# Delivering most of the input already transposed by DMA, behind the first weights, in a linear-attention and GEGLU kernel

## The chip, the cores and the metric

The kernel runs on one core of a Trainium2 chip. The metric is the device time of one execution in microseconds (us), as the median of several executions; all runs compared here are of the same ("fast") state unless the text says otherwise. The profiled execution's span is about 1.7 us shorter than its device time.

## The reference, cut to what matters

```python
S, D, H, F = 2048, 640, 32, 1728           # tokens, width, heads, FFN width; all bf16
g = sigmoid((x * gate_w).sum(-1, keepdims=True))
# A: linear attention
q, k, v = split_heads(x @ wqkv)            # head dim 20
phi = lambda t: where(t > 0, t + 1, exp(t)) + 1e-6
kv, z = sum_s(phi(k) v^T), sum_s(phi(k))   # over ALL tokens
a = ((phi(q) @ kv) / (phi(q) . z)) @ wo
# B: GEGLU
b = (gelu(x @ w_gate) * (x @ w_up)) @ w_down
out = g * a + (1 - g) * b
```

Every product contracts over the width D, so x is needed with D on the partitions: x transposed (`xT`, 5 blocks of 128 by 2048 tokens). The K and V projections of all 16 token tiles come first, because kv and z sum over all tokens.

## The kernel before

It is a hand-scheduled program: `op`, `mmg` and `dma` issue an instruction on an engine and insert semaphore waits from a table of readers and writers. x is cut in four chunks of 512 tokens. All loads go through one queue, that of SyncE (SP).

```python
for q in range(4):                                   # 4 x 640 KB, natural layout
    dma([], [r_xnat[q]], (sem_x[q], 16), ... x_nat[:, 4*q:4*q+4, :] <- x2[q*512:(q+1)*512, :] ...)
dma(... gwrow <- gate_w ...)                         # 1.2 KB
dma([], [r_wkv], (sem_wkv, 16), ... wkv_sb <- A_wqkv[:, D:3*D] ...)   # 1600 KB
for q in range(4): sp.wait_ge(sem_x[q], 16)
# ... then wo, wq, w_gate, w_up, w_down (8 MB) ...

for gi, (c, k) in enumerate(tgroups):                # 4 chunks x 5 blocks, 8 PSUM banks in turn
    bank = gi % 8
    mmg([r_xnat[c], r_ident], [r_bank[bank]], [4 transposes 128x128 into pt (bf16 PSUM)])
    op(DV, [r_bank[bank]], [r_xT[k][c]], lambda e: e.tensor_copy(xT[:, k, c*512:(c+1)*512], pt[...]))
# ... gate_w transposed the same way ...

for t in range(NT):                                  # 16 token tiles: the KV phase
    # 3 groups (512, 512, 256 columns) x 5 matmuls into banks 3*(t%2) .. 3*(t%2)+2
    mmg(xT_chunk(t // TPC) + [r_wkv], banks3, emits)
    # ScalarE: exp and relu of K, copy of V;  VectorE: min, add -> pk_sb, v_sb
    if t == 3:
        emit_gate_row()                              # 20 matmuls, reads ALL of xT
# then: mask matmuls into banks 4, 5, 6;  kv^T = 5 x 16 matmuls;  z;  q;  W2;  FFN and output, 4 chunks
```

## Time and profile before

| | before |
|---|---|
| median of runs | 331.55 us (330.78 to 333.22, 16 runs) |
| profiled span | 329.7 us |
| TensorE busy | 313.5 us, 95% of the span |
| first TensorE instruction | 5.09 us |
| first KV matmul | 14.95 us |

The page's row of slices first (the span in 40 equal parts, each 8.2 us; a digit is the busy share in tenths, `PEclk` the granted TensorE clock in tenths, `GB/s` what the DMA engines moved).

```profile
...
PE   3699999799999999999999999999999999999996
...
PEclk9999999999899999999999999999999999999999
DMA  7999300000000000000000000000000100000001
GB/s 255 379 392 388 111 1 1 2 2 0 0 2 0 0 1 3 35 27 20 0 2 0 0 22 20 34 9 1 1 2 0 40 22 20 0 3 1 20 22 40
DMA packets 9489, 15.46 MB, mean 47 GB/s; under 512 B 442, under 2 KB 7546, under 8 KB 9466
...
```

Four slices of TensorE are not nearly full: the first two (3 and 6), the eighth (7), and the last (6), the end of the kernel. The DMA engines are busy in the first four slices only. From the third slice on the kernel is mostly bound by TensorE, so only the start can be gained by a change to the loads. The timeline of the start says what happens there (columns: start, duration in us, engine, line, operation, output <- input, number merged, and in brackets the idle time before it with what ended it).

```profile
...
0.80 2.43 SPq L292 DMA_DIRECT2D x_nat<-in_A_x_dram  x4
...
3.79 0.38 SPq L311 DMA_DIRECT2D wkv_sb<-in_A_wqkv_dram  x1
...
5.09 6.89 PE L354 MATMUL pt<-ident,x_nat 128*128 128x128 bf16 x80 [5.09 <-DMA x_nat<-in_A_x_dram]
5.74 7.67 DVE L360 COPY xT<-pt 128x512 bf16<-128x512 bf16 x20 [5.74 <-PE pt L354]
...
14.95 10.76 PE L435 MATMUL ps<-wkv_sb,xT 128*128 128x512 bf16 x58 [2.87 <-DMA wkv_sb<-in_A_wqkv_dram]
17.64 0.70 ACT L445 ACTIVATE e1k<-ps 128x640 bf16<-128x640 f32 x1 [15.56 <-PE ps L435]
...
```

The four x loads are issued at 0.80 us, wkv (`L311`) at 3.79 us. The transposes start when the first x chunk has landed (5.09 us) and end at 11.98 us. Then TensorE idles for 2.87 us until wkv has landed, and the KV phase starts at 14.95 us. The chain of waits (followed back from the last instruction; start, duration, what) agrees:

```profile
...
3.79 10.81 DMA wkv_sb<-in_A_wqkv_dram
...
```

wkv takes 10.81 us from issue to landing, because 2.6 MB of x are ahead of it in the queue.

### The profile page before, as it was taken

To read this page: it belongs to the slowest core of one execution; us is meant where nothing else is said; L and a number is where in the kernel's file an instruction comes from. 1 tells how busy PE (TensorE), PEld (TensorE's weight loads), DVE (VectorE), ACT (ScalarE), POOL (GpSimd) and SP (SyncE) were. 2 spreads that over 40 slices of the span, in tenths; PEclk is the share of its full clock that TensorE was granted. 3 is DMA by queue.
4 is the path that set the end of the run, shared out by engine and by line. 5 is a ranking of instruction groups with operands and counts; after the bars stand their busy time and mean duration, and the time that the engine had idled before them with its cause. 6 is when DMAs were issued, how large, how long until landed. Compare 5 with 4: busy or idle time off the path is not lost.

```text
span 329.7 us, 4747 instructions
## 1 busy us (share of the span) xinstructions
PE 313.5 (95%) x1795; PEld 168.9 (51%) x1819; DVE 192.0 (58%) x320; ACT 165.9 (50%) x318; POOL 73.5 (22%) x64
## 2 busy tenths in 40 slices
PE   3699999799999999999999999999999999999996
PEld 3555555554444445564444555544445564444664
DVE  3625222216869995712999954079995712999400
ACT  1067677618577873104777600267873105777111
POOL 8000000000026540000654300026540000666000
PEclk9999999999899999999999999999999999999999
DMA  7999300000000000000000000000000100000001
GB/s 255 379 392 388 111 1 1 2 2 0 0 2 0 0 1 3 35 27 20 0 2 0 0 22 20 34 9 1 1 2 0 40 22 20 0 3 1 20 22 40
DMA packets 9489, 15.46 MB, mean 47 GB/s; under 512 B 442, under 2 KB 7546, under 8 KB 9466
## 3 DMA queue, kind: packets, MB, share of 16 engines
q1 hardware_dynamic: 9466, 15.16, 12.7%
q8 instruction: 14, 0.23, 0.3%
q14 instruction: 9, 0.07, 0.1%
HBM read 12.54 MB, written 2.62 MB: 46 GB/s over the span
## 4 chain that ended last, share of the span: by engine, by line
PE 78%; DVE 7%; issue 6%; ACT 4%; DMA 3%; SPq 1%; ACTq 0%; DVEq 0%
PE ps L736 20%; PE ps L637 14%; PE ps L435 13%; PE ps L643 12%; PE ps L727 7%; PE ps L467 5%; DMA wkv_sb<-in_A_wqkv_dram 3%; DVE t L680 3%; ACT xh L657 2%; PE ps L551 2%; PE ps L596 1%; PE ps L561 1%; PE ps L497 1%; DVE inner L664 1%; ACT rq L475 1%
## 5 line engine op out<-in xcount | busy, mean ns | idle before, releaser
L688 POOL TENSOR_TENSOR uT<-u,omg_bc 128x512 bf16<-128x512 bf16 x48 | 66.0, 1374 | 225.4 <-DVE u L684 225.4
L664 DVE SCALAR_TENSOR_TENSOR inner<-sq,xh 128x512 bf16<-128x512 bf16 (+1 forms) x56 | 49.4, 882 | 44.2 <-ACT xh L657 43.9
L736 PE MATMUL ps<-wd_sb,uT 128*128 128x320 bf16 x448 | 73.2, 300 | 0.2
L643 PE MATMUL ps<-xT,wu_sb 128*128 128x512 bf16 (+1 forms) x277 | 68.9, 379 | 0.2
L637 PE MATMUL ps<-xT,wg_sb 128*128 128x512 bf16 (+1 forms) x272 | 68.0, 379 | 0.9 <-issue 0.5
L736 PEld LDWEIGHTS ps<-wd_sb,uT 128*128 128x128 bf16 x448 | 42.8, 97 | 26.2 <-issue 4.2
L752 ACT ACTIVATE out_sb<-ps 128x320 bf16<-128x320 f32 x32 | 12.2, 434 | 83.5 <-PE ps L736 83.5
L654 ACT ACTIVATE sq<-ps 128x512 bf16<-128x512 f32 (+1 forms) x56 | 33.4, 596 | 29.7 <-PE ps L637 27.1
L435 PE MATMUL ps<-wkv_sb,xT 128*128 128x512 bf16 (+1 forms) x235 | 43.2, 343 | 3.1 <-DMA wkv_sb<-in_A_wqkv_dram 2.9
L643 PEld LDWEIGHTS ps<-xT,wu_sb 128*128 128x128 bf16 (+1 forms) x280 | 27.6, 99 | 32.8
L637 PEld LDWEIGHTS ps<-xT,wg_sb 128*128 128x128 bf16 (+1 forms) x280 | 27.0, 99 | 33.6 <-ACT sq L654 1.7
L680 DVE SCALAR_TENSOR_TENSOR t<-th,ps 128x512 bf16<-128x512 bf16 (+1 forms) x56 | 37.9, 676 | 0.0
L672 ACT ACTIVATE th<-inner 128x512 bf16<-128x512 bf16 (+1 forms) x56 | 35.3, 630 | 1.0 <-DVE inner L664 1.0
L435 PEld LDWEIGHTS ps<-wkv_sb,xT 128*128 128x128 bf16 x240 | 23.3, 98 | 22.9 <-issue 2.7
L657 ACT ACTIVATE xh<-ps 128x512 bf16<-128x512 f32 (+1 forms) x56 | 33.1, 591 | 0.0
L684 DVE TENSOR_TENSOR u<-t,xh 128x512 bf16<-128x512 bf16 (+1 forms) x56 | 30.0, 535 | 1.9
L727 PE MATMUL ps<-W_sb,pqnT 128*128 128x320 bf16 x160 | 27.0, 299 | 0.0
L445 ACT ACTIVATE e1k<-ps 128x640 bf16<-128x640 f32 x16 | 11.2, 703 | 27.3 <-PE ps L435 27.3
L467 PE MATMUL ps<-xT,wq_sb 128*128 128x512 bf16 x96 | 22.8, 379 | 0.6 <-issue 0.6
L454 DVE TENSOR_SCALAR emk<-e1k 128x640 bf16<-128x640 bf16 x16 | 5.2, 327 | 26.2 <-ACT e1k L445 26.2
L727 PEld LDWEIGHTS ps<-W_sb,pqnT 128*128 128x128 bf16 x160 | 15.7, 98 | 6.1
L480 DVE TENSOR_TENSOR pqT<-emq,rq 128x512 bf16<-128x512 bf16 x20 | 16.1, 807 | 2.0 <-ACT rq L475 1.3
(68 smaller groups left out, 203.2 us busy)
## 6 DMA issues: line engine op xcount, KB each, us to landing
x_nat<-in_A_x_dram SPq DMA_DIRECT2D x4, 640.0 KB, 6.2
out_dram<-out_sb SPq DMA_DIRECT2D x16, 160.0 KB, 1.8
wg_sb<-in_B_w_gate_dram SPq DMA_DIRECT2D x1, 2160.0 KB, 14.5
wu_sb<-in_B_w_up_dram SPq DMA_DIRECT2D x1, 2160.0 KB, 19.4
wd_sb<-in_B_w_down_dram SPq DMA_DIRECT2D x1, 2080.0 KB, 21.7
wkv_sb<-in_A_wqkv_dram SPq DMA_DIRECT2D x1, 1600.0 KB, 10.8
wo_sb<-in_A_wo_dram SPq DMA_DIRECT2D x1, 800.0 KB, 6.3
wq_sb<-in_A_wqkv_dram SPq DMA_DIRECT2D x1, 800.0 KB, 8.1
```

Of the source, the lines that this page charges most:

```text
L435: emits.append(lambda e, base=base, coff=coff, width=width, t=t, k=k: e.matmul(ps[:, base + coff: base + coff + width], lhsT=xT[:, k, t * ...
L467: [lambda e, k=k, i=i, qb=qb: e.matmul(bank_ap(qb), lhsT=wq_sb[:, k, 128 * i:128 * (i + 1)], rhs=xT[:, k, c0:c0 + CH], start=(k == 0), sto ...
L637: [lambda e, k=k, Mj=Mj, f0=f0, gb=gb: e.matmul(bank_ap(gb, p1=Mj), lhsT=wg_sb[:, k, f0:f0 + Mj], rhs=xT[:, k, c0:c0 + CH], start=(k == 0) ...
L643: [lambda e, k=k, Mj=Mj, f0=f0, ub=ub: e.matmul(bank_ap(ub, p1=Mj), lhsT=wu_sb[:, k, f0:f0 + Mj], rhs=xT[:, k, c0:c0 + CH], start=(k == 0) ...
L654: lambda e, Mj=Mj, gb=gb, sl=sl: e.activation(sq[0:Mj, sl, :], bank_ap(gb, p1=Mj), ACT.Square, scale=SQ_SCALE))
L657: lambda e, Mj=Mj, gb=gb, sl=sl: e.activation(xh[0:Mj, sl, :], bank_ap(gb, p1=Mj), ACT.Copy, scale=0.5))
L664: lambda e, Mj=Mj, sl=sl: e.scalar_tensor_tensor(out=inner[0:Mj, sl, :], in0=sq[0:Mj, sl, :], scalar=1.0, in1=xh[0:Mj, sl, :], op0=ALU.add ...
L672: lambda e, Mj=Mj, sl=sl: e.activation(th[0:Mj, sl, :], inner[0:Mj, sl, :], ACT.Tanh, scale=2.0 * GELU_C))
L680: lambda e, Mj=Mj, ub=ub, sl=sl: e.scalar_tensor_tensor(out=t2[0:Mj, sl, :], in0=th[0:Mj, sl, :], scalar=1.0, in1=bank_ap(ub, p1=Mj), op0= ...
L688: lambda e, Mj=Mj, sl=sl, jf=jf, cb=cb: e.tensor_tensor(uT[0:Mj, cb, jf, :], u1[0:Mj, sl, :], omg_bc[0:Mj, c0:c0 + CH], ALU.mult))
L727: lambda e, i=i, bank=bank, coff=coff, mi=mi, cb=cb, tok0=tok0: e.matmul(bank_ap(bank, n=HALF_D), lhsT=pqnT[:, cb, i, tok0:tok0 + 128], rh ...
L736: lambda e, jf=jf, Mj=Mj, bank=bank, coff=coff, mi=mi, cb=cb, tok0=tok0: e.matmul(bank_ap(bank, n=HALF_D), lhsT=uT[0:Mj, cb, jf, tok0:tok0 ...
```

## The change

Its intent: wkv goes ahead of three of the four x chunks; these three come from DRAM already transposed (a transposing DMA straight into `xT`), so TensorE and VectorE transpose only chunk 0. 81 dummy matmuls bridge TensorE's waiting times so that its clock is not lowered. The gate row, which needs all of `xT`, moves from tile 3 to tile 7.

```diff
-for q in range(4): dma(... x_nat chunk q ...)
-dma(gwrow);  dma(wkv)
+dma([], r_W2[0:TPC], (sem_x[0], 16), ... W2_sb[:, 0:4, :] <- x2[0:CH, :] ...)   # chunk 0, natural
+dma(wkv)
+dma(gwrow)
+for c in range(1, NCH):                                   # chunks 1 to 3
+    dma([], [r_xT[k][c] for k in range(KT)], (sem_x[c], 16),
+        lambda e, c=c: e.dma_start_transpose(xT[:, :, c*CH:(c+1)*CH], x2[c*CH:(c+1)*CH, :]))
 for q in range(NCH): sp.wait_ge(sem_x[q], 16)
 # ... wo, wq, w_gate, w_up, w_down as before ...
-for c, k in tgroups (20): 4 transposes into bf16 PSUM, one VectorE copy
+45 dummy matmuls (ident x ident, 128x128) into bank 6
+for k in range(KT):                                       # chunk 0 only: plain matmuls by ident, fp32 PSUM
+    mmg(r_W2[0:TPC] + [r_ident], [r_bank[k]], [4 matmuls lhsT=W2_sb[:, j, k*128:(k+1)*128], rhs=ident])
+    op(DV, [r_bank[k]], [r_xT[k][0]], ... tensor_copy(xT[:, k, 0:CH], bank_ap(k)))
+36 dummy matmuls into bank 6
 # gate_w transposed (now a plain matmul)
 ...
-            if t == 3:
+            if t == 7:
                 emit_gate_row()
```

More of the change, by code (lines that the diff above doesn't have):

```diff
@@ L285, in _build @@
     with nc.Block():
-        xa_x_nat = nc.sbuf_tensor("x_nat", [128, NT, D], dt.bfloat16, side="right")
-        xa_gwrow = nc.sbuf_tensor("gwrow", [KT, 128], dt.bfloat16, side="right")
-        xa_pt = nc.psum_tensor("pt", [128, 8192], dt.bfloat16)
-        with xa_x_nat as x_nat, xa_gwrow as gwrow, xa_pt as pt:
-            for q in range(4):
-                dma([], [r_xnat[q]], (sem_x[q], 16),
-                    lambda e, q=q: e.dma_start(
-                        x_nat[:, 4 * q:4 * q + 4, :],
-                        x2[q * 512:(q + 1) * 512, :].rearrange("(t p) d -> p t d", p=128)))
-            dma([], [r_gwrow], (sem_gw, 16),
-                lambda e: e.dma_start(gwrow[:], gate_w.rearrange("(k p) -> k p", p=128)))
-            esP = ExitStack()
-            esP.__enter__()
-            pk_sb = esP.enter_context(nc.sbuf_tensor("pk_sb", [128, NT, D], dt.bfloat16))
-            v_sb = esP.enter_context(nc.sbuf_tensor("v_sb", [128, NT, D], dt.bfloat16))
-            e1k = esP.enter_context(nc.sbuf_tensor("e1k", [128, 2, D], dt.bfloat16))
-            rk = esP.enter_context(nc.sbuf_tensor("rk", [128, 2, D], dt.bfloat16))
-            emk = esP.enter_context(nc.sbuf_tensor("emk", [128, 2, D], dt.bfloat16))
-            zr_sb = esP.enter_context(nc.sbuf_tensor("zr_sb", [1, D], dt.float32))
-            maskT = esP.enter_context(nc.sbuf_tensor("maskT", [128, KT, 160], dt.bfloat16))
-            KVT_bd = esP.enter_context(nc.sbuf_tensor("KVT_bd", [128, KT, D], dt.bfloat16))
-            wkv_sb = esP.enter_context(nc.sbuf_tensor("wkv_sb", [128, KT, 2 * D], dt.bfloat16))
-            dma([], [r_wkv], (sem_wkv, 16),
-                lambda e: e.dma_start(wkv_sb[:], A_wqkv[:, D:3 * D].rearrange("(k p) f -> p k f", p=128)))
-            for q in range(4):
-                sp.wait_ge(sem_x[q], 16)
-            sp.wait_ge(sem_gw, 16)
-            dma([], [r_wo], (sem_wo, 16),
-                lambda e: e.dma_start(wo_sb[:], A_wo.rearrange("(k p) f -> p k f", p=128)))
-            dma([], [r_wq], (sem_wq, 16),
-                lambda e: e.dma_start(wq_sb[:], A_wqkv[:, 0:D].rearrange("(k p) f -> p k f", p=128)))
-            dma([], [r_wg], (sem_wg, 16),
-                lambda e: e.dma_start(wg_sb[:], B_w_gate.rearrange("(k p) f -> p k f", p=128)))
-            dma([], [r_wu], (sem_wu, 16),
-                lambda e: e.dma_start(wu_sb[:], B_w_up.rearrange("(k p) f -> p k f", p=128)))
-            dma([], [r_wd[0]], (sem_wd, 32),
-                lambda e: e.dma_start(wd_sb[:, 0:FB - 1, :],
-                                      B_w_down[0:(FB - 1) * 128, :].rearrange("(k p) f -> p k f", p=128)))
-            dma([], [r_wd[1]], (sem_wd, 32),
-                lambda e: e.dma_start(wd_sb[0:F - (FB - 1) * 128, FB - 1, :],
-                                      B_w_down[(FB - 1) * 128:F, :]))
-            op(PO, [], [r_ident], lambda e: e.memset(ident[:], 0.0))
-            op(PO, [], [r_ident], lambda e: e.affine_select(
-                out=ident[:], in_=ident[:], compare_op=ALU.not_equal, fill=1.0,
-                base=0, pattern=[[-1, 128]], channel_multiplier=1))
-            op(PO, [], [r_ones], lambda e: e.memset(ones_col[:], 1.0))
-            op(PO, [], [r_ones], lambda e: e.memset(onesF[:], 1.0))
-            op(PO, [], [r_ones], lambda e: e.memset(onesB[:], 1.0))
-            op(PO, [], [r_Ez], lambda e: e.memset(E_sb[:], 0.0))
-            op(PO, [r_Ez], [r_E], lambda e: e.memset(E_sb[0:32, :], 1.0))
-            op(PO, [], [r_E], lambda e: e.affine_select(
-                out=E_sb[0:32, :], in_=E_sb[0:32, :], compare_op=ALU.is_ge, fill=0.0,
-                base=0, pattern=[[1, D]], channel_multiplier=-DH))
-            op(PO, [], [r_E], lambda e: e.affine_select(
-                out=E_sb[0:32, :], in_=E_sb[0:32, :], compare_op=ALU.is_ge, fill=0.0,
-                base=(DH - 1), pattern=[[-1, D]], channel_multiplier=DH))
-            op(PO, [], [r_KVTbd_z], lambda e: e.memset(KVT_bd[:], 0.0))
-            op(PO, [], [r_Zbz], lambda e: e.memset(Zb[:], 0.0))
-            tgroups = [(c, k) for c in range(NCH) for k in range(KT)]
-            for gi, (c, k) in enumerate(tgroups):
-                bank = gi % 8
-                emits = []
-                for j in range(TPC):
-                    t = TPC * c + j
-                    emits.append(lambda e, bank=bank, j=j, t=t, k=k: e.transpose(
-                        pt[:, bank * 1024 + j * 128: bank * 1024 + (j + 1) * 128],
-                        x_nat[:, t, k * 128:(k + 1) * 128],
-                        ident[:]))
-                mmg([r_xnat[c], r_ident], [r_bank[bank]], emits)
-                op(DV, [r_bank[bank]], [r_xT[k][c]],
-                   lambda e, bank=bank, k=k, c=c: e.tensor_copy(
-                       xT[:, k, c * 512:(c + 1) * 512],
-                       pt[:, bank * 1024:bank * 1024 + 512]))
-            gwb = len(tgroups) % 8
-            mmg([r_gwrow, r_ident], [r_bank[gwb]],
-                [lambda e: e.transpose(pt[:, gwb * 1024:gwb * 1024 + KT], gwrow[0:KT, :], ident[0:KT, 0:KT])])
-            op(DV, [r_bank[gwb]], [r_gw],
-               lambda e: e.tensor_copy(gw_sb[:, :], pt[:, gwb * 1024:gwb * 1024 + KT]))
-            snapA = snapshot()
@@ L374, in bank_ap, with emit_xT_dma @@
             return ps[p0:p1, b * 512 + lo:b * 512 + lo + n]
+        def emit_xT_dma(c):
+            dma([], [r_xT[k][c] for k in range(KT)], (sem_x[c], 16),
+                lambda e, c=c: e.dma_start_transpose(
+                    xT[:, :, c * CH:(c + 1) * CH],
+                    x2[c * CH:(c + 1) * CH, :]))
+        gwrow = es.enter_context(nc.sbuf_tensor("gwrow", [KT, 128], dt.bfloat16, side="right"))
+        x_nat = W2_sb[:, 0:TPC, :]
+        dma([], r_W2[0:TPC], (sem_x[0], 16),
+            lambda e: e.dma_start(x_nat, x2[0:CH, :].rearrange("(t p) d -> p t d", p=128)))
@@ new lines, in _build @@
+        esP = ExitStack()
+        esP.__enter__()
+        pk_sb = esP.enter_context(nc.sbuf_tensor("pk_sb", [128, NT, D], dt.bfloat16))
+        v_sb = esP.enter_context(nc.sbuf_tensor("v_sb", [128, NT, D], dt.bfloat16))
+        e1k = esP.enter_context(nc.sbuf_tensor("e1k", [128, 2, D], dt.bfloat16))
+        rk = esP.enter_context(nc.sbuf_tensor("rk", [128, 2, D], dt.bfloat16))
+        emk = esP.enter_context(nc.sbuf_tensor("emk", [128, 2, D], dt.bfloat16))
+        zr_sb = esP.enter_context(nc.sbuf_tensor("zr_sb", [1, D], dt.float32))
@@ new lines, in _build @@
+        maskT = esP.enter_context(nc.sbuf_tensor("maskT", [128, KT, 160], dt.bfloat16))
+        KVT_bd = esP.enter_context(nc.sbuf_tensor("KVT_bd", [128, KT, D], dt.bfloat16))
+        wkv_sb = esP.enter_context(nc.sbuf_tensor("wkv_sb", [128, KT, 2 * D], dt.bfloat16))
+        dma([], [r_wkv], (sem_wkv, 16),
+            lambda e: e.dma_start(wkv_sb[:], A_wqkv[:, D:3 * D].rearrange("(k p) f -> p k f", p=128)))
+        dma([], [r_gwrow], (sem_gw, 16),
+            lambda e: e.dma_start(gwrow[:], gate_w.rearrange("(k p) -> k p", p=128)))
@@ new lines, in _build @@
+        for c in range(1, NCH):
+            emit_xT_dma(c)
+        for q in range(NCH):
+            sp.wait_ge(sem_x[q], 16)
+        sp.wait_ge(sem_gw, 16)
+        dma([], [r_wo], (sem_wo, 16),
+            lambda e: e.dma_start(wo_sb[:], A_wo.rearrange("(k p) f -> p k f", p=128)))
+        dma([], [r_wq], (sem_wq, 16),
+            lambda e: e.dma_start(wq_sb[:], A_wqkv[:, 0:D].rearrange("(k p) f -> p k f", p=128)))
+        dma([], [r_wg], (sem_wg, 16),
+            lambda e: e.dma_start(wg_sb[:], B_w_gate.rearrange("(k p) f -> p k f", p=128)))
@@ new lines, in _build @@
+        dma([], [r_wu], (sem_wu, 16),
+            lambda e: e.dma_start(wu_sb[:], B_w_up.rearrange("(k p) f -> p k f", p=128)))
+        dma([], [r_wd[0]], (sem_wd, 32),
+            lambda e: e.dma_start(wd_sb[:, 0:FB - 1, :],
+                                  B_w_down[0:(FB - 1) * 128, :].rearrange("(k p) f -> p k f", p=128)))
+        dma([], [r_wd[1]], (sem_wd, 32),
+            lambda e: e.dma_start(wd_sb[0:F - (FB - 1) * 128, FB - 1, :],
+                                  B_w_down[(FB - 1) * 128:F, :]))
@@ new lines, in _build @@
+        op(PO, [], [r_ident], lambda e: e.memset(ident[:], 0.0))
+        op(PO, [], [r_ident], lambda e: e.affine_select(
+            out=ident[:], in_=ident[:], compare_op=ALU.not_equal, fill=1.0,
+            base=0, pattern=[[-1, 128]], channel_multiplier=1))
+        op(PO, [], [r_ones], lambda e: e.memset(ones_col[:], 1.0))
+        op(PO, [], [r_ones], lambda e: e.memset(onesF[:], 1.0))
+        op(PO, [], [r_ones], lambda e: e.memset(onesB[:], 1.0))
+        op(PO, [], [r_Ez], lambda e: e.memset(E_sb[:], 0.0))
@@ new lines, in _build @@
+        op(PO, [r_Ez], [r_E], lambda e: e.memset(E_sb[0:32, :], 1.0))
+        op(PO, [], [r_E], lambda e: e.affine_select(
+            out=E_sb[0:32, :], in_=E_sb[0:32, :], compare_op=ALU.is_ge, fill=0.0,
+            base=0, pattern=[[1, D]], channel_multiplier=-DH))
+        op(PO, [], [r_E], lambda e: e.affine_select(
+            out=E_sb[0:32, :], in_=E_sb[0:32, :], compare_op=ALU.is_ge, fill=0.0,
+            base=(DH - 1), pattern=[[-1, D]], channel_multiplier=DH))
+        op(PO, [], [r_KVTbd_z], lambda e: e.memset(KVT_bd[:], 0.0))
@@ new lines, in _build @@
+        op(PO, [], [r_Zbz], lambda e: e.memset(Zb[:], 0.0))
+        mmg([r_ident], [r_bank[6]],
+            [lambda e: e.matmul(ps[:, 3072:3200], lhsT=ident[:], rhs=ident[:],
+                                start=True, stop=True) for _ in range(45)])
+        for k in range(KT):
+            mmg(r_W2[0:TPC] + [r_ident], [r_bank[k]],
+                [lambda e, j=j, k=k: e.matmul(
+                    bank_ap(k, lo=j * 128, n=128),
+                    lhsT=W2_sb[:, j, k * 128:(k + 1) * 128], rhs=ident[:],
+                    start=True, stop=True) for j in range(TPC)])
+            op(DV, [r_bank[k]], [r_xT[k][0]],
+               lambda e, k=k: e.tensor_copy(xT[:, k, 0:CH], bank_ap(k)))
@@ new lines, in _build @@
+        mmg([r_ident], [r_bank[6]],
+            [lambda e: e.matmul(ps[:, 3072:3200], lhsT=ident[:], rhs=ident[:],
+                                start=True, stop=True) for _ in range(36)])
+        mmg([r_gwrow, r_ident], [r_bank[7]],
+            [lambda e: e.matmul(ps[:, 3584:3584 + KT], lhsT=gwrow[0:KT, :], rhs=ident[0:KT, 0:KT],
+                                start=True, stop=True)])
+        op(DV, [r_bank[7]], [r_gw],
+           lambda e: e.tensor_copy(gw_sb[:, :], ps[:, 3584:3584 + KT]))
@@ L376, in _build @@
+        snapA = snapshot()
         pqT = es.enter_context(nc.sbuf_tensor("pqT", [128, 2, KT, CH], dt.bfloat16, side="right"))
```

## The prediction

> What bounds the kernel now. TensorE is busy 313.5 of 329.7 us (busy table) and holds 78% of the chain of waits; no DMA matters after 40 us (row of forty slices). Only the first 15 us are not matmul work. The timeline shows there: the first transpose at 5.09 us, when the first 640 KB of x landed; 80 TensorE transposes until 11.98 us, paced by 20 VectorE copies (7.67 us in all); then TensorE idle for 2.87 us until 14.95 us, "DMA wkv_sb". The chain names the same piece: wkv, issued at 3.79 us, lands 10.81 us later, because it queues behind all four x loads (2.6 MB). From 14.95 us on the KV phase runs at 2.70 us per token tile (tile ends on ScalarE at 17.64, 20.34, 23.05 us), to 60.1 us.
>
> What the change does. Only chunk 0 of x is loaded plainly; wkv goes second in the queue; chunks 1 to 3 arrive by transposing DMA straight into xT. It removes 60 transposes and 15 copies, and adds 81 dummy matmuls that keep TensorE's clock up. The chunk-0 transposes become ordinary matmuls into fp32 PSUM, whose copies should cost about 0.6 us each instead of 0.38 (estimate from the 0.68 us of a 512-element fp32 PSUM operation, line 503). The gate row moves from after tile 3 to after tile 7; its work stays the same (1.9 us on TensorE).
>
> Cost on the critical path. The new start of KV is the latest of three:
> - wkv landing: chunk 0 still lands at about 5.0 us; 1.64 MB more at the 360 to 400 GB/s that the x and wkv loads show gives about 9.3 us (gate_w shortly after it);
> - the five copies: first transposes done at 5.4 to 6.8 us, plus 5 x 0.6, 8.5 to 9.8 us;
> - TensorE: 45 dummies from about 1.6 us at 65 to 107 ns (the 140-column matmuls take 65 ns a piece, line 551) end at 4.5 to 6.4 us; 20 transposes 1.7 us; 36 dummies about 2.3 us: 9 to 10.4 us.
> So KV starts at about 9.8 instead of 14.95 us: 5 us saved, and everything after it, which is bound by TensorE, shifts as a whole.
>
> The transposing DMAs have deadlines: chunk 1 at tile 4 (about 20.6 us), chunks 2 and 3 both at the gate row (about 31.5 us). The Trainium skill, "DMA: Bandwidth & Descriptors", section "Latency and other measured facts", gives 261 GB/s for a DMA transpose with a non-contiguous middle dimension; by it 2.5 us a chunk, all landed by 17 to 18 us (estimate). Even three times slower they would land by about 32 us. No transposing DMA is in this trace to compare. The other weights are issued only after them, and needed 27 us of loading before; wq is first used at 72.5 us, so this slack suffices.
>
> Predicted: 331.4 - 5 = 326.5 us; range 325.0 to 333.0. Faster by over 2% 0.10, within 2% 0.77, slower by over 2% 0.13. To pass 2% KV would have to start before 8.4 us, which wkv's bytes hardly allow.
>
> What would show it: the first KV matmul at 9.3 to 10.5 us; KV tiles at 2.70 us throughout, with no wait of TensorE on a DMA into xT at tiles 4 or 8 or at the gate row; transposing DMAs of 2.5 to 7 us each; from the KV phase on, the same durations as before.
>
> What would make it wrong: transposing DMAs below about 90 GB/s (TensorE waits at tile 4 or the gate row, and the loss could be tens of us); transposes sharing the rings with wkv and delaying it; a cold TensorE clock at the KV start; dummies that overrun the data.

## The result, and the profile after

The changed kernel takes 326.29 us in the median (325.74 to 328.49, 11 runs), against 331.55 us (16 runs) before. The ratio is 0.9855, 95% interval 0.983 to 0.988: 1.4% faster. (Ratios are the mean time of one kernel's fast runs over that of the other's fast runs of the same rounds, so they are not quite the ratio of the medians quoted. The record lists a twelfth execution of the changed kernel, 325.66 us, that its summary leaves out; it changes nothing here.)

The same rows of the page, after:

```profile
...
PE   8999998999999999999999999999999999999996
...
PEclk9999999798999999999999999999999999999999
DMA  7979910000000000100000000100000100000001
GB/s 267 207 235 403 378 50 2 1 2 0 0 2 0 1 2 1 40 22 20 0 2 0 0 22 20 43 0 1 1 2 0 42 20 20 2 1 0 23 20 40
DMA packets 15681, 15.46 MB, mean 47 GB/s; under 512 B 8170, under 2 KB 13738, under 8 KB 15658
...
```

TensorE's first two slices are 8 and 9 now (dummies included). The DMA engines move only 207 and 235 GB/s in the second and third slice, where the transposing DMAs run. The clock row shows lower digits in the eighth and the tenth slice, of which more below. The timeline of the start:

```profile
...
0.80 0.46 SPq L300 DMA_DIRECT2D W_sb<-in_A_x_dram  x1
...
1.32 0.49 SPq L315 DMA_DIRECT2D wkv_sb<-in_A_wqkv_dram  x1
...
1.58 4.98 PE L358 MATMUL ps<-ident 128*128 128x128 bf16 x45 [1.58 <-POOL ones_col L343]
...
2.37 13.98 SPq L293 DMA_TRANSPOSE xT<-in_A_x_dram  x3
...
6.35 1.55 PE L362 MATMUL ps<-ident,W_sb 128*128 128x128 bf16 x20
7.02 3.08 DVE L367 CAST xT<-ps 128x512 bf16<-128x512 f32 x5 [7.02 <-PE ps L362]
...
7.74 2.17 PE L370 MATMUL ps<-ident 128*128 128x128 bf16 x36
...
10.39 21.58 PE L438 MATMUL ps<-wkv_sb,xT 128*128 128x512 bf16 x117 [0.37 <-DVE gw_sb L376]
13.07 0.70 ACT L448 ACTIVATE e1k<-ps 128x640 bf16<-128x640 f32 x1 [11.00 <-PE ps L438]
...
```

wkv is issued at 1.32 us and lands 7.9 us later by the list of DMA issues, at 9.2 us, and no longer holds anything up. The start of KV, 10.39 us, is now set by TensorE and VectorE: 45 dummies until 6.56 us, the transposes after them, and five copies of 0.68 us (3.08 us in all) from 7.02 to 10.10 us. The chain of waits of the changed kernel has the same three pieces:

```profile
...
1.58 4.98 PE ps L358 x45
6.56 0.44 PE ps L362 x4
...
7.02 3.08 DVE xT L367 x5
...
```

The transposing DMAs cost TensorE nothing. What waited for them is only the queue's own wait before the other weights, which ended at about 18.5 us (view of the waits of SP; columns: who, for whom, us in total, times, longest):

```profile
...
SPq L322 <- DMA xT<-in_A_x_dram: 2.1, 1, 2.1
...
```

Chunk 3 is needed at the gate row only, at 31.9 us. They are slower than plain loads, though. The view of stretches (busy us of each engine with its count, then granted clock, DMA share and, last, GB/s) gives 356 GB/s while chunk 0 and wkv arrive, and 196 GB/s while only transposing DMAs run, with the DMA engines as busy (share 0.99):

```profile
...
2.50:9.20 6.70, 6.70 (x86) 6.70 (x84) 2.18 (x4) 0.00 (x0) 5.47 (x6) 1.00 1.04 356
9.30:18.40 9.10, 8.73 (x57) 5.04 (x56) 2.56 (x7) 3.79 (x6) 0.53 (x1) 1.00 0.99 196
...
```

The kernel before had 371 GB/s over its x and wkv loads (2.5 to 14.5 us in the same view). The packet line of the page, shown above for both, says what differs: packets under 512 B rise from 442 to 8170, by 7728, and 1.97 MB in pieces of 256 B would be 7680. That the small packets are the reason for the lower rate was not tested.

**Where the profiles disagree with the medians.** The profiled spans differ by 3.0 us only (329.7 and 326.7), though KV starts 4.56 us earlier and the KV phase itself is as long (ScalarE's last evacuations start at 60.14 and 55.58 us, 4.56 us apart). The chains show where the rest went: 80 matmuls of kv^T, right after the KV phase, took 5.11 us before and 6.70 us after. That is all of it: from ScalarE's last evacuation to the end of the span there are 269.6 us before and 271.1 us after, 1.6 us more.

```profile
...
62.77 5.11 PE ps L551 x80
...
```

```profile
...
58.21 6.70 PE ps L554 x80
...
```

The stretches show why. First the kernel before, then the changed one; the third number from the right is the granted clock.

```profile
...
62.00:64.00 2.00, 1.82 (x32) 1.77 (x33) 0.14 (x2) 1.23 (x11) 0.00 (x0) 1.00 0.03 8
64.00:66.00 2.00, 2.00 (x34) 2.00 (x32) 0.53 (x3) 0.28 (x3) 0.00 (x0) 1.00 0.00 0
...
```

```profile
...
58.00:60.00 2.00, 2.00 (x22) 1.92 (x20) 0.00 (x0) 1.47 (x10) 0.00 (x0) 0.53 0.01 4
60.00:62.00 2.00, 2.00 (x23) 2.00 (x22) 0.41 (x2) 0.00 (x0) 0.00 (x0) 0.62 0.00 0
...
80.00:82.00 2.00, 2.00 (x10) 1.06 (x8) 2.00 (x1) 1.24 (x4) 0.00 (x0) 0.50 0.00 0
...
```

The changed kernel's profile ran at 0.53 and 0.62 of the clock just there, and a second time at 78 to 82 us. The profile before had the second dip only (80 to 86 us). These dips come and go between executions of one and the same kernel, and they fit the spread of the times (only one run of each kernel has a trace, but every run has its mean clock; what decides when a dip comes is taken up under e8). The changed kernel's times fall in two groups, 325.7 to 326.3 and 328.1 to 328.5 us, with mean clocks of 0.995 to 0.999 and 0.990 to 0.993; the kernel before has 330.8 to 331.7 and 332.5 to 333.2 us. The profiled run of the changed kernel (328.45 us) lies in its upper group, that of the kernel before (331.4 us) in its lower one. Compared floor to floor, the gain is 330.78 - 325.74 = 5.0 us.

### The profile page after: what moved, and what is told of

Its sections match the earlier page's. It is cut to its first block, busy times and chain, and to the rows that moved or that the text cites. A ratio compares the mean times of both kernels' runs of the same rounds, so it can differ in the third digit from the quotient of the medians.

```text
span 326.7 us, 4772 instructions
## 1 busy us (share of the span) xinstructions
PE 316.6 (97%) x1816; PEld 171.9 (53%) x1840; DVE 187.4 (57%) x305; ACT 165.9 (51%) x318; POOL 73.7 (23%) x64
## 2 busy tenths in 40 slices
DMA packets 15681, 15.46 MB, mean 47 GB/s; under 512 B 8170, under 2 KB 13738, under 8 KB 15658
## 4 chain that ended last, share of the span: by engine, by line
PE 81%; DVE 8%; issue 6%; ACT 4%; ACTq 0%; POOL 0%; POOLq 0%; DVEq 0%
PE ps L739 21%; PE ps L640 14%; PE ps L438 13%; PE ps L646 12%; PE ps L730 7%; PE ps L470 5%; DVE t L683 3%; PE ps L554 2%; ACT xh L660 2%; PE ps L358 2%; PE ps L599 1%; PE ps L564 1%; PE ps L500 1%; DVE inner L667 1%; ACT rq L478 1%
## 5 line engine op out<-in xcount | busy, mean ns | idle before, releaser
L457 DVE TENSOR_SCALAR emk<-e1k 128x640 bf16<-128x640 bf16 x16 | 5.2, 327 | 25.3 <-ACT e1k L448 25.2
```

## The experiments

All gave correct results. Times are listed by the two groups (execution without, or with, the dip after the KV phase, as the mean clock and the profiles suggest; e8's groups are of another kind, see there); "first evacuation" is when ScalarE starts on the first KV tile. The kernel before ran beside each, with floors of 330.83 to 330.88 us. Each experiment starts from the changed kernel unless its section names another. "First KV matmul" is the first that the trace recorded. In most profiles the very first record is missing, and the first weight load of KV came 0.2 to 0.3 us earlier (14.71 us before, 10.16 changed, 9.60 in e5); in e4 and e7b it is not missing (weight loads at 9.48 and 11.09 us), so starts are compared below by the weight load where that matters.

| run | lower group us | upper group us | ratio to before | first KV matmul | first evacuation |
|---|---|---|---|---|---|
| before | 330.8 to 331.7 | 332.5 to 333.2 | 1 | 14.95 | 17.64 |
| changed | 325.7 to 326.3 | 328.1 to 328.5 | 0.9855 | 10.39 | 13.07 |
| e1 order only | 328.8 to 329.4 | 331.5 | 0.9917 | 9.63 | 12.31 |
| e2 wkv last | 339.1, 339.3 | | 1.0209 | 20.91 | 25.77 |
| e3 gate row at tile 3 | 325.7, 325.9 | 327.8, 328.0 | 0.9833 | 10.21 | 12.90 |
| e4 no dummies | 327.9 to 328.7 | 330.6 | 0.9878 | 9.48 | 15.04 |
| e5 trimmed dummies | 325.6 | 327.6 to 327.9 | 0.9848 | 9.87 | 12.56 |
| e6 wkv in three pieces | 324.3 | 325.8 to 325.9 | 0.9792 | 7.51 | 10.85 |
| e7b all four chunks by DMA | 327.7, 327.9 | 329.1, 329.2 | 0.9881 | 11.12 | 14.02 |
| e8 e6 and the gap after KV closed | 321.5 | 322.3 to 322.5 | 0.9690 | 8.41 | 11.10 |

### e1: the load order without the transposing DMAs

The theory: two things are needed together. The order lets KV start early, and the transposing DMAs keep 60 transposes off TensorE that the long wait for wkv had hidden before. The rival: the order alone does it.

```diff
-    emit_xT_dma(c)                       # chunks 1 to 3
+    emit_x_load(c)                       # natural, into w_down's still empty tile
...
+            if t < 12:                   # transposes of the next chunk between the KV tiles
+                for k in [[0, 1], [2, 3], [4], []][t % TPC]:
+                    emit_xT_group(t // TPC + 1, k)
-            if t == 7:
+            if t == 12:
                 emit_gate_row()
```

(w_down is loaded after the KV phase in this kernel, so that its tile can hold x meanwhile.)

> The changed kernel's load order (chunk 0, wkv, then the rest), but chunks 1 to 3 are loaded plainly and transposed on TensorE, one or two groups after each KV tile, with the gate row after tile 12. My theory: the start of KV moves to about 10.4 us because of the order alone, but the 60 transposes come back onto TensorE's path inside the KV phase at 65 to 77 ns each, 3.9 to 4.6 us, so the time is 330 to 331 us, the gain nearly all lost. Rival: the gain is the shorter queue ahead of wkv and the TensorE transposes were never the limit; then 326 to 327 us.

Measured: 328.76 us at best, ratio 0.9917. KV started as early as in the changed kernel (9.63 us), but the transposes now lie between its tiles (`L308`; timeline of TensorE):

```profile
...
9.63 2.65 PE L450 MATMUL ps<-wkv_sb,xT 128*128 128x512 bf16 x14 [0.37 <-DVE gw_sb L388]
12.11 0.61 PE L308 MATMUL ps<-ident,wd_sb 128*128 128x128 bf16 x8
12.56 2.87 PE L450 MATMUL ps<-wkv_sb,xT 128*128 128x512 bf16 x15
...
```

Eight of them take 0.45 us (12.11 to 12.56 us), 56 ns each, and the next KV tile waits for as long. Floor to floor the order alone brings 330.85 - 328.76 = 2.1 us, and the transposing DMAs the other 328.76 - 325.74 = 3.0 us. The traces show the same without the floors: from the first KV matmul to ScalarE's last evacuation (58.16 us in e1) the KV phase takes 48.5 us in e1 and 45.2 us in both other kernels, 3.3 us longer, which is 60 times 56 ns. So the theory holds in kind, but my 65 to 77 ns a transpose was too much, and e1 ended about 1 us below the range expected for it. The rival, 326 to 327 us, is out.

### e2: wkv behind the transposing DMAs

```diff
-dma(wkv)                                 # second in the queue
 for c in range(1, NCH): emit_xT_dma(c)
+dma(wkv)
```

> wkv is issued after the three transposing DMAs instead of before them, nothing else. My theory: the gain hangs on wkv going ahead; the transposing DMAs hold the issuing queue for about 14 us, so wkv is issued at about 16.4 us, lands at about 21 us, KV starts at about 21 us instead of 10, and the time is 335 to 338 us, slower than the kernel before. Rival: transposing DMAs are fast enough that their place in the queue matters little; then 326 to 329 us.

Measured: 339.05 and 339.33 us (two runs), 2.1% slower than the kernel before (interval 1.7 to 2.5%). Timeline of TensorE:

```profile
...
20.91 3.62 PE L438 MATMUL ps<-wkv_sb,xT 128*128 128x512 bf16 x8 [11.33 <-DMA wkv_sb<-in_A_wqkv_dram]
```

and of the issuing queue:

```profile
...
13.43 0.59 SPq L320 DMA_DIRECT2D wkv_sb<-in_A_wqkv_dram  x1
...
```

TensorE waits 11.33 us for wkv. The three transposing DMAs occupied the issuing queue from 1.81 to 13.39 us (its timeline shows 11.58 us for the three), so wkv was not even issued before 13.43 us. The time is above the range expected because TensorE came out of the long idle time at a low clock: the trace grants it 0.50 from 11.7 to 25.3 us, and the first tile took 4.86 us (20.91 to 25.77) instead of 2.69. The gain of the change hangs on the order.

### e3: the gate row back at tile 3

```diff
-            if t == 7:
+            if t == 3:
```

> Only the gate row goes back to after tile 3. The last transposing DMA landed at about 18.5 us and tile 3 ends at about 21.2 us, so my theory expects no wait and no change: within 0.5 us of the changed kernel. Rival: the move was needed because the gate row reads all four chunks; then TensorE waits on xT for some us before tile 4.

Measured: 325.66 us at best against 325.74 us, both groups as in the changed kernel. The gate row ran at 20.91 us with no wait for `xT`:

```profile
...
20.91 1.90 PE L394 MATMUL ps<-xT,gw_sb 128*1 128x512 bf16 x20
...
```

So this part of the change was not needed; the last chunk is there before tile 3 ends.

### e4: no dummy matmuls

```diff
-45 dummy matmuls (before the transposes of chunk 0)
-36 dummy matmuls (after them)
```

> All 81 dummy matmuls taken out. My theory: the 45 first dummies ran cold (110 ns each) until 6.55 us and held back the chunk-0 transposes by 1.3 us, so without them the transposes start at 5.1 us and KV starts at about 9.4 us, but on a cold TensorE: some 3 us of KV at half speed cost 1.5 us, so the time is 325.8 to 327.5 us, a wash. Rival (the change's intent): the dummies pay for themselves; without them 1.5 us or more are lost.

Measured: 327.92 us at best, 2.2 us more than the changed kernel. TensorE's timeline and, below it, the chain:

```profile
...
5.09 2.31 PE L359 MATMUL ps<-ident,W_sb 128*128 128x128 bf16 x20 [5.09 <-DMA W_sb<-in_A_x_dram]
...
9.48 6.86 PE L432 MATMUL ps<-wkv_sb,xT 128*128 128x512 bf16 x20
```

```profile
...
9.55 8.41 PE ps L432 x30
...
```

KV did start earlier, at 9.48 us (0.7 us before the changed kernel by the weight loads; the loads set the start: wkv landed at 9.2 us and gate_w, which is transposed before KV, at 9.3), but the first 30 matmuls (two tiles) took 8.41 us, where 2 x 2.70 = 5.4 us are usual: 3.0 us lost. ScalarE starts on the second tile at 18.00 us instead of 15.78, 2.2 us later, as much as the floors differ. My theory had the mechanism and half the size; the rival, that the dummies pay for themselves, is right. The Trainium skill, "TensorE: Matmul & The Clock Gate", Part 1, describes it: the clock is halved by default, about 107 ns for a 128-column matmul, and released by some 3.4 us of activity seen in a window that runs freely. The first 45 dummies take 4.98 us in the changed kernel (111 ns each), the later 36 take 2.17 us (60 ns each). A free-running window fits this as well: the same 45 took 3.96 us in e3 and 4.60 us in e7b. The list of clock changes that each trace keeps seems to begin at the release: at 6.90 us in the changed kernel, 4.28 in e3, 5.64 in e7b and only 15.41 in e4, where the two slow tiles are.

### e5: fewer first dummies, gate_w out of the way

```diff
-... for _ in range(45)])
+... for _ in range(33)])                 # first dummies
-... for _ in range(36)])
+... for _ in range(43)])                 # second dummies
-# gate_w transposed before KV
+            if t == 6: (gate_w transposed here)
```

> 33 instead of 45 first dummies, 43 instead of 36 second ones, and the transpose of gate_w moved to after tile 6. In the runs so far TensorE waited before KV for gate_w (0.4 to 2.0 us) or for the copies, never for wkv itself. My theory: KV starts right when wkv lands, 9.2 to 9.4 us, still on a warm clock: 0.5 to 1.0 us less than the changed kernel, so about 325 to 325.5 us where no clock dip follows. Rival: with fewer first dummies the clock is released later and part of KV runs cold; then nothing is gained.

Measured: 325.64 us at best, 0.1 us below the changed kernel's floor: nothing gained that can be told from the spread.

```profile
...
5.09 2.33 PE L362 MATMUL ps<-ident,W_sb 128*128 128x128 bf16 x20
7.21 2.62 PE L370 MATMUL ps<-ident 128*128 128x128 bf16 x43
9.87 14.33 PE L433 MATMUL ps<-wkv_sb,xT 128*128 128x512 bf16 x77
```

The transposes started at once when x had landed (5.09 us), but 20 of them took 2.33 us instead of 1.55 us, because the clock was still low; and the 43 second dummies overran wkv's landing (9.1 us). The rival was half right: what the shorter warm-up saved, the transposes lost.

### e6: wkv in three pieces

```diff
-dma([], [r_wkv], (sem_wkv, 16), ... all 1280 columns ...)
+for gi, (coff, width) in enumerate(kv_groups):       # 512, 512, 256 columns
+    dma([], [r_wkv3[gi]], (sem_wkv3[gi], 16), ... columns coff to coff+width ...)
-    tensor_copy of all five blocks on VectorE
+    blocks 0, 2, 4 on VectorE, blocks 1, 3 on ScalarE
-    mmg(xT_chunk(t // TPC) + [r_wkv], banks3, emits)
+    mmg([], banks3, emits)       # each matmul waits for its own block of xT and its own piece of wkv
```

(On top of e5, with 4 second dummies instead of 43.)

> As e5, with wkv loaded in three column pieces under semaphores of their own, the chunk-0 copies shared by VectorE and ScalarE, tile 0 waiting block by block, and 4 second dummies. If the start of KV is bound by wkv's bytes (1.64 MB at 360 to 400 GB/s), the first 0.66 MB suffice for the first third of tile 0: KV starts at about 7 us, tile 0 ends at about 10.1 us instead of 13.1, and the time is 323 to 324 us where no clock dip follows. Rival: pieces with shorter runs load more slowly, and nothing is gained over e5.

Measured: 324.25 us at best, ratio 0.9792. Timeline of TensorE:

```profile
...
7.51 1.03 PE L443 MATMUL ps<-wkv_sb,xT 128*128 128x512 bf16 x4 [0.34 <-ACT xT L378]
9.01 15.21 PE L443 MATMUL ps<-wkv_sb,xT 128*128 128x512 bf16 x83 [0.47 <-DMA wkv_sb<-in_A_wqkv_dram]
```

KV starts at 7.51 us, waits 0.47 us for a later piece, and the first tile is done at 10.85 us, 1.7 us before e5's (12.56). The floor fell by 1.4 us, the upper group by 1.8 us. The last piece landed only at about 10.0 us (issued at about 2.4 us, 7.6 us to landing), later than the whole wkv in e5 (9.1 us), but it is needed last. e6 changes several things at once (three pieces, fewer dummies, shared copies, waits by block), so the 1.4 us are not divided among them. What its trace does show is that a start at 7.51 us rests on the pieces: the first landed at 7.0 us, and a wait for the whole wkv, which landed at 9.1 us in e5, would not have allowed it. The prediction's remark that wkv's bytes hardly allow a start before 8.4 us holds, as far as these runs show, only for wkv under one semaphore.

### e7 and e7b: all four chunks by transposing DMA

> Chunk 0 is transposed by DMA too, first in the queue, and TensorE transposes nothing of x (66 instead of 36 second dummies keep it warm). From the 211 GB/s that I read off the changed kernel's trace (1.97 MB between 9.2 and 18.5 us): chunk 0 at 6.4 us, wkv behind it at 10.6 us, KV starts at about 10.9 us, 326.3 to 327.3 us. Rival: a transposing DMA at the head of the queue holds back wkv's issue by its own issue time (3.3 to 7.1 us) and its 10.6 us from issue to landing; then KV starts at 13 us or later, and the time is 329 us or more.

The profile of e7 fell in an execution of 415.88 us at a granted clock of 0.75 from about 8 us to the end, which no other run shows and which I can't explain; its fast runs took 327.46, 327.47 and 331.83 us (ratio 0.9896). In that profile wkv landed at 11.0 us, but the 66 dummies had overrun it.

```diff
-dma(chunk 0, natural into W2_sb);  20 transposes and 5 copies of chunk 0
+emit_xT_dma(0)                           # first in the queue
 # e7b: on top of e5, with 45 and 60 dummies
```

> As e7, whose one profile fell in a slow execution and whose last dummies, not wkv, set the start of KV: now with 60 instead of 66 second dummies and with gate_w out of the way as in e5. In e7 wkv landed at 11.0 us (1.7 us after the changed kernel's). My theory: KV starts at 11.0 to 11.4 us, so 326.5 to 327 us where no clock dip follows, 1 to 1.5 us more than e5: transposing chunk 0 on TensorE is the better choice, because its plain load is the faster one. Rival: with VectorE's and TensorE's chunk-0 work gone the start is as early as e5's and the times agree.

Measured: 327.68 us at best, 2.0 us more than e5 and 0.7 us above the range expected. wkv landed at 10.95 us (issued at 3.55 us, behind 2.69 us of issue time of the first transposing DMA), and TensorE waited for it:

```profile
...
11.12 9.13 PE L422 MATMUL ps<-wkv_sb,xT 128*128 128x512 bf16 x49 [1.59 <-DMA wkv_sb<-in_A_wqkv_dram]
```

KV starts 1.5 us after e5's (weight loads at 11.09 and 9.60 us), and chunk 0 is better transposed by TensorE. The two profiles, which both have the dip after the KV phase and a mean clock of 0.993, differ by the same 1.5 us (329.19 and 327.65 us), 1.45 of them there already at the last KV tile. The floors differ by 0.5 us more; e5's floor is a single run, and I leave that rest open.

### e8: a version that beats both

In all profiles so far TensorE idles for about 2.1 us after the last KV tile: the mask matmuls that come next write banks that ScalarE is still emptying. In the changed kernel the clock dip at 58 to 62 us follows it:

```profile
...
57.62 0.17 PE L529 MATMUL ps<-ident,E_sb 32*128 32x32 bf16 x1 [2.08 <-ACT v_sb L454]
...
```

```diff
-mask matmuls after the KV phase, into banks 4, 5, 6
+mask matmuls before the KV phase, into banks 6, 7
-for j in range(5): kv^T group j over tiles 0..15
+for j in range(3): kv^T group j over tiles 0..14     # needs nothing of tile 15
+for j in range(3): kv^T group j, tile 15
+for j in 3, 4:     kv^T group j over tiles 0..15
```

(On top of e6.)

> As e6, with the mask matmuls moved to before KV and the KV-transpose groups of tiles 0 to 14 put ahead of tile 15's, so that the 2.1 us in which TensorE waits for ScalarE's evacuation of the last KV tile are filled. If this idle time is what lets the granted clock fall to a half right after it in some runs (58 to 62 us in the changed kernel's profile, 1.6 us lost), then that dip is gone in all runs and the time is 320.5 to 322 us. If the dip has another cause, two groups of times about 2 us apart remain.

Measured: 321.9 us in the median (321.45 to 322.52, 6 runs), ratio to the kernel before 0.969 (0.9665 to 0.9715): 3.1% faster than it, and floor to floor 2.8 us faster than e6. kv^T (`L564`) now follows the KV phase without a gap and takes 5.16 us at a full clock (timeline and stretches):

```profile
...
49.72 4.06 PE L468 MATMUL ps<-wkv_sb,xT 128*128 128x512 bf16 x23
53.61 5.16 PE L564 MATMUL ps<-pk_sb,v_sb 128*128 128x140 bf16 x80
...
```

```profile
...
54.00:56.00 2.00, 2.00 (x36) 2.00 (x34) 0.82 (x2) 1.71 (x3) 0.00 (x0) 1.00 0.04 8
...
72.00:74.00 2.00, 2.00 (x9) 1.05 (x8) 1.18 (x2) 0.14 (x1) 0.00 (x0) 0.56 0.03 8
...
```

The dip after the KV phase is gone in this profile, and no run of the six lies 2 us above the floor, as 5 of 11 did in the changed kernel. A smaller split of 1.0 us remains: the profiled run (322.33 us, upper group) has the other dip at 72 to 76 us. e5's profile is the counterpart: it has the dip at 58 to 62 us (0.63, 0.52), a clock of 1.00 at 78 to 82 us, and 2.0 us more than e5's floor.

e8 fills the gap and moves the matmuls in one edit, and only one of its six runs has a trace; in the other five the absence of the dip is read from their times. The clock changes kept in the traces add what e8 alone leaves open. In all profiles but e7's, every dip lasts 3.41 us (e2's long one four times that), and the stretch between two changes is a whole multiple of it (51.20 and 17.07 us in the changed kernel). So the clock changes on a grid of 3.41 us, which lies differently in each execution. Laid over the gap after the KV phase, in stretches of 0.1 us: where 1.65 to 2.08 us of it fell in one step of the grid (changed, e3, e4, e5, e6, e7b), the next step ran at half the clock; where the grid cut it in two (0.95 and 1.12 us in the kernel before, 0.83 and 1.24 in e1, 1.44 and 0.64 in e2), no dip followed. So the gap, and where the grid cuts it, fit the dip after the KV phase in all nine profiles that have the gap, and its coming and going. The other dip, at 72 to 86 us, follows a step with only 0.30 us of idle time; its cause stays open.

## Why the prediction was right or wrong, point by point

The prediction was right: 326.5 us foretold, 326.29 us measured, in the range and in the class it favoured. That the two numbers agree within 0.2 us is partly luck: six of the eleven runs lie in the lower group and the median is the highest of them; with one more in the upper group it would have been 328.07 us. And in the profiles the start of KV moved by 4.6 us, not by 5.

- *Only the first 15 us can be gained, because wkv queues behind x.* Right. e2 puts wkv behind the other three chunks again and loses more than the gain; the start of KV carries through to the end (4.56 us at the first KV matmul, 4.56 us at the last KV tile).
- *wkv lands at about 9.3 us.* Right: 9.2 us.
- *KV starts at about 9.8 us.* The profiled run had 10.39 us (weight load 10.16), inside the 9.3 to 10.5 us given. The copies came last, as one of the three terms of the sum, and ended at 10.10 us instead of 8.5 to 9.8. What was mis-sized is the 45 dummies ahead of them: I allowed 65 to 107 ns each, and they ran at 111 ns here (88 to 111 ns over the runs), ending at 6.56 us (5.5 to 6.6), so the first transposes were done at 7.00 us and not at 5.4 to 6.8. The copies were sized rightly: each takes 0.68 us, but they overlap, and five take 3.08 us where I had 3.0. In e1, e3 and e4, where TensorE and the copies were done sooner, the loads set the start: wkv landed at 9.3, 9.6 and 9.2 us, and in e3 and e4 gate_w, behind it in the queue and transposed before KV, at 9.8 and 9.3 us.
- *The transposing DMAs meet their deadlines.* Right, with a wrong rate. The 261 GB/s of the skill's page became 196 GB/s here, so they had landed by 18.5 us instead of 17 to 18. The deadlines were 20.6 and 31.5 us. e3 shows that even a deadline at tile 3 would have been met.
- *60 transposes and 15 copies are removed.* I listed this and gave it no value. e1 shows that it is worth 3.0 of the 5.0 us (floor to floor; 3.3 us of TensorE time in the trace), because under the new order they would no longer be hidden. A sum that prices only the new start would have promised the same 5 us to e1, which reached 2.1.
- *Dummies keep the clock up.* Right, and worth 2.2 us (e4). One reading in the prediction was wrong, without harm to the number: in the kernel before, the 80 transposes were not paced by VectorE. Until 9.8 us they start every 107 ns and after that about every 60 ns, and the trace's list of clock changes begins at 9.85 us. So they ran at the low clock and, while TensorE waited for wkv anyway, warmed it as the dummies do now; that is inferred from these numbers.
- *From the KV phase on, the same durations as before.* Wrong for the profiled run: kv^T took 6.70 instead of 5.11 us at a clock of 0.53 to 0.62. Apart from that dip it holds (269.6 us from the last KV tile to the end before, 271.1 after, 1.6 of them kv^T). I had not asked whether the times before already formed two groups.

## What to carry to other kernels

Before moving a load forward, ask which work its long wait had been hiding: that work comes onto the critical path unless the same change takes it away. A transposing DMA is a good place for such work when it stands behind the urgent loads in the queue and well ahead of its first use; at the head of the queue it delays the others by its bytes and by its issue time. Where the times of one kernel form groups, look for the clock in each profile before explaining a difference between two of them, and close an idle gap that stands just before the dip, if there is one.

## What the Trainium skill lacked or had wrong

- "DMA: Bandwidth & Descriptors", section "Latency and other measured facts": 261 GB/s for a DMA transpose with a non-contiguous middle dimension. Here three blocks of 512 x 640, transposed from DRAM one after the other, ran at 196 GB/s (192 in e2), against 356 and 371 GB/s of plain loads (changed kernel and kernel before). The source blocks are contiguous in DRAM here, their places in `xT` are not.
- "Advanced Engine Details and Errata", section "X-Bar Transpose (TRN2)": says that transposing DMAs are as fast as regular ones, 350 to 400 GB/s. Not in this case, as above.
- None of the pages has the issue time of a transposing DMA of this size (the DMA page has a cycle count for small tiles only). One of 640 KB holds the issuing queue for 2.7 us when it is first (e7b), for 3.1 to 3.7 us in most other places and for up to 7.1 us behind wkv. A plain load of the same size took 0.43 to 0.5 us at the head of the queue, 0.86 us as the fourth in a row and up to 2.4 us behind wkv (e1). Everything after it in the queue waits that long.
- "TensorE: Matmul & The Clock Gate", Part 1, gives the rule that TensorE should have no idle gaps above some 3.4 us. Here a shorter one was enough: the gap of 2.1 us between the KV phase and the mask matmuls was followed by a half clock in six profiles and not in three, according to how much of it fell in one step of the clock's grid, and the dip vanished with the gap (e8).
- The same page, Part 4, gives about 275 to 390 ns for a transpose on TensorE in its transpose mode, which is the duration of one. It lacks what one costs in a stream, where they overlap: as plain matmuls by an identity they take 219 ns each by the trace and cost 56 ns each (e1: 3.3 us for 60).
- No page says that a profile's granted clock does not show the cold start (the page on TensorE warns only in general that clock events can be unreliable): in the changed kernel it reads 1.00 in the first 6 us, where 45 matmuls took 111 ns each, almost twice the later 60 ns.
